# Cosine layer of a fused attention kernel: a step's seven products in one run and its twelve rows in the next, VectorE's chain work moved to the rows

## The chip, the cores and the metric

The kernel runs on one core of a Trainium2 chip. The metric is the device time of one execution in microseconds (us); before the change the median of three runs is 984.97 us (984.43 to 987.22). TensorE multiplies (PE in the profile, its weight loads PEld), VectorE (DVE) and ScalarE (ACT) work elementwise, GpSimd (POOL) too but only on SBUF, and SyncE (SP) issues the transfers.

## What is computed

```python
def reference(q, k, v, w_gate, w_val, w_out, w_in2, w_out2):
    x = sliding_window_attention(q, k, v)        # 4 x 8 heads, 576 tokens, window 128
    x = x.reshape(2304, 512)
    x = (silu(x @ w_gate) * (x @ w_val)) @ w_out # 512 -> 1536 -> 512
    h = x @ w_in2                                # 512 -> 2048: the cosine layer
    return ((h * cos(h)) @ w_out2).astype(float32)
```

All of it is float32. The kernel splits every operand of a product into a high and a low part and sums three matmuls (high x high, high x low, low x high).

## The kernel before

The kernel has three stages: attention (to about 230 us of the profile), the gated layer (to about 600 us) and the cosine layer (the last 380 us). The change touches the cosine layer alone.

**Steps.** The 2304 tokens are cut into NS = 3 stretches s of 768 columns, each stretch into two halves of 384. The 2048 columns of `w_in` are taken in 8 pairs p (NPAIR) of two blocks of 128. A step k = 8 s + p computes four blocks of h, (fi, half), from seven **products** m = 0 to 6 in place of eight (a scheme of the Strassen kind: the sums of inputs are made beforehand by `make_xt`, those of outputs by `take`). A product (`prod`, L1030 to L1032) is six matmuls of 384 columns, so a step has 42 of them. There are 24 steps, k = 0 to 23.

**Banks.** From the twelfth product on, a product writes one of the two banks of PSUM that the pool `pm` has (L196, `new_bank` L1114); product 6 goes on adding in the bank of product 4. So product m needs what product m - 2 left there to have been read.

**Emptying** (`take`, L1175, and `add`, L1171). Product 0 is copied by ScalarE (L1181), every other one is added to an earlier sum by VectorE (L1171). Four of the seven results, those of m = 1, 4, 5 and 6, are a finished block of h and start a **chain**.

**Chains** (`cosine`, L1142, a generator). One chain turns one block of 128 x 384 into h cos(h), high and low, in six parts: two operations of ScalarE that round (L1145, L1146); two of VectorE that give the remainder r (L1149, L1150); absolute value and sine on ScalarE (L1152, L1153); a multiplication on GpSimd (L1155); the high part on ScalarE (L1159); the low part on VectorE (L1161). `slot_chains` takes every living chain one part further after each product.

**Rows** (`out_rows`, L1206). The blocks of step k are multiplied by `w_out` in step k + 2: 12 rows (fi, j), each three matmuls of 512 columns (L84 to L86), 36 a step, which add into six banks over all eight steps of a stretch. The list `PER` says how many rows follow each product:

```python
    PER = [2, 2, 2, 2, 2, 1, 1]
```

**Inputs of the next stretch.** `make_xt` (L979) makes the seven inputs, high and low, of stretch s + 1 from the tile `raw`: operations 768 wide on ScalarE (L994), VectorE and GpSimd (both L991). In the kernel before they stand in a list `bg`, of which one is issued after each product from p = 3, m = 3 on. This happens twice, in steps 3 to 6 and 11 to 14.

**Queues.** Every engine runs its instructions in the order in which the program issues them; there is no planner here, so the order of the Python calls is the order of the engines. SyncE's queue carries the 256 KB of weights of each product (`load_ws`, seven buffers, seven products ahead), the two tiles of 512 KB for the rows (`load_wo`) and the outputs.

Of the kernel before, what the change touches and what calls it, by code (L numbers as in the profile page):

```python
# [13 lines left out]
ALU = mybir.AluOpType  # L14
# [14 lines left out]
def kernel(  # L29
# [50 lines left out]
    def f32(ap):  # L80
        return ap.bitcast(F32)
# [100 lines left out]
    post = deque()  # L182
# [25 lines left out]
    def flush():  # L208
        for _ in range(len(post)):
            post.popleft()()  # L210
# [768 lines left out]
    def make_xt(s, pool, raw):  # L979

        hi = [pool.tile([128, 2, BW], F32R, tag=f"xh{m}", name=f"xh{m}") for m in range(7)]
        lo = [pool.tile([128, 2, BW], F32R, tag=f"xl{m}", name=f"xl{m}") for m in range(7)]
        XT[s] = hi, lo
        b11, b12 = raw[:, 0:2, 0:BW], raw[:, 0:2, BW:SB]
        b21, b22 = raw[:, 2:4, 0:BW], raw[:, 2:4, BW:SB]

        src = [b11, b21, b11, b22, b12, b22, b21]
        v, g = nc.vector, nc.gpsimd

        def two(eng, out, a, b, op=ALU.subtract):  # L990
            return lambda: eng.tensor_tensor(out=out, in0=a, in1=b, op=op)  # L991

        def high(m):
            return lambda: nc.scalar.copy(out=hi[m], in_=src[m])  # L994

        def low(eng, m):
            return two(eng, lo[m], src[m], f32(hi[m]))
        return [
            high(0), high(1), two(g, b12, b22, b12), low(v, 0), low(v, 1), high(5), two(v, b11, b12, b11, ALU.add),
            low(g, 5), two(v, b21, b21, b11), high(2), high(4), two(g, b22, b22, b11), low(v, 2), high(6), low(v, 4),  # L1000
            high(3), low(v, 6), low(g, 3)]
# [140 lines left out]
    def cosine(k, fi, half, h):  # L1142

        a = ap_.tile([128, BW], F32, tag="a", name="a")
        nc.scalar.activation(out=a, in_=h, func=AF.Copy, scale=INV2PI, bias=MAGIC)  # L1145
        nc.scalar.activation(out=a, in_=a, func=AF.Copy, bias=-MAGIC)  # L1146
        yield
        r = rp.tile([128, BW], F32, tag="r", name="r")
        nc.vector.scalar_tensor_tensor(out=r, in0=a, scalar=-C1, in1=h, op0=ALU.mult, op1=ALU.add)  # L1149
        nc.vector.scalar_tensor_tensor(out=r, in0=a, scalar=-C2, in1=r, op0=ALU.mult, op1=ALU.add)  # L1150
        yield
        nc.scalar.activation(out=r, in_=r, func=AF.Abs)  # L1152
        nc.scalar.activation(out=r, in_=r, func=AF.Sin, bias=halfpi, scale=-1.0)  # L1153
        yield
        nc.gpsimd.tensor_tensor(out=r, in0=r, in1=h, op=ALU.mult)  # L1155
        yield
        hi = hp.tile([128, BW], F32R, tag="hh", name="hh")
        lo = hp.tile([128, BW], F32R, tag="hl", name="hl")
        nc.scalar.copy(out=hi, in_=r)  # L1159
        yield  # L1160
        (nc.vector if k else nc.gpsimd).tensor_tensor(out=lo, in0=r, in1=f32(hi), op=ALU.subtract)  # L1161
        HS[k, fi, half] = hi, lo

    def slot_chains(most):

        for c in list(live)[:most]:
            if next(c, "end") == "end":
                live.remove(c)

    def add(out, a, ps):  # L1170
        nc.vector.tensor_tensor(out=out, in0=ps[:, :BW], in1=a, op=ALU.add)  # L1171
# [3 lines left out]
    def take(k, m, ps):  # L1175

        def new(pool, tag):
            return pool.tile([128, BW], F32, tag=tag, name=tag)
        if m == 0:
            cur[k, "q"] = new(tp, "q")  # L1180
            nc.scalar.copy(out=cur[k, "q"], in_=ps[:, :BW])  # L1181
        elif m == 1:
            c = new(cp, "c")
            add(c, cur[k, "q"], ps)
            live.append(cosine(k, 0, 0, c))
        elif m == 2:
            add(cur[k, "q"], cur[k, "q"], ps)
        elif m == 3:
            cur[k, "r"] = new(tp, "r5")
            add(cur[k, "r"], cur[k, "q"], ps)  # L1190
        else:
            c = new(cp, "c")
            fi, half, base = {4: (1, 1, "r"), 5: (0, 1, "r"), 6: (1, 0, "q")}[m]
            add(c, cur[k, base], ps)
            live.append(cosine(k, fi, half, c))

    def load_wo(k):
        if k < K2:
# [3 lines left out]
                WO[k, fi] = t  # L1202

    sums = {}

    def out_rows(k, fi, j):  # L1206

        s, p = divmod(k, NPAIR)
        first, final = p == 0 and fi == 0, p == NPAIR - 1 and fi == 1
        if first:  # L1210
            sums[j] = (pl2.tile([128, 512], F32, tag="l2", name="l2") if j < 5 else
                       pl1a.tile([128, 512], F32, tag="l1", name="l1"))
        hi, lo = HS[k, fi, j // 3]
        w = WO[k, fi]
        c = slice(j % 3 * 128, (j % 3 + 1) * 128)
        mm3(sums[j], hi[:, c], lo[:, c], w[:, 0], w[:, 1], first, final)
        if final:
            def ev(ps=sums[j], row=s * 6 + j):
                o = op_.tile([128, 512], F32, tag="o", name="o")
                if j % 2 and s == NS - 1:  # L1220
                    nc.vector.tensor_copy(out=o, in_=ps)
                else:
                    nc.scalar.copy(out=o, in_=ps)
                nc.sync.dma_start(out=out[row * 128:(row + 1) * 128, :], in_=o)
            post.append(ev)

    raws = {}

    def load_raw(s):
        raws[s] = raw_p.tile([128, KD, SB], F32, tag="raw", name="raw")  # L1230
        nc.sync.dma_start(out=raws[s], in_=y2d[s])

    PER = [2, 2, 2, 2, 2, 1, 1]
    rows = deque()
    bg = deque()
    p7 = {}
    for at, (k, m) in enumerate(order):
        if k >= 2 and m == 0:
            pairs = [(fi, j) for fi in range(2) for j in range(6)]
            rows += [(k - 2, fi, j) for fi, j in (sorted(pairs, key=lambda x: x[1]) if k == K2 + 1 else pairs)]  # L1240
        if k < K2:
            if k == 0 and m < 2:
                ps = bank0[m]
            elif m == 6:
                ps = p7.pop(k)
                prod(k, m, ps, start=False)
            else:
                ps = new_bank(6 * k + m)
                prod(k, m, ps)
            if m == 4:  # L1250
                p7[k] = ps
        slot_chains(2 if k < 2 else 99)
        flush()
        if bg:
            bg.popleft()()
        if k < K2:
            take(k, m, ps)
        for _ in range(PER[m]):
            if rows:
                out_rows(*rows.popleft())  # L1260
        if k < K2:
            load_ws(at + 8)
        if m == 1:
            load_wo(k - 1 if k else K2)
        s, p = divmod(k, NPAIR)
        if k == 1 and m == 3:
            load_raw(1)
        if m == 3 and s + 1 < NS and p == 3:
            bg += make_xt(s + 1, xta if s % 2 else xtb, raws[s + 1])
        if m == 3 and s + 2 < NS and p == 6:  # L1270
            load_raw(s + 2)
    flush()
    sc.close()
    pre.close()
# [31 lines left out]
```

## Time and profile before

| | us |
|---|---|
| median of three runs | 984.97 (984.43 to 987.22) |
| the profiled execution, its own time | 982.86 |
| span of its profile | 981.1 |
| PE busy in the span | 958.9 (98%) |
| DVE, ACT, POOL busy | 735.7, 591.7, 483.8 |
| the chain that ended last: PE's share | 90% |

The span begins at the first instruction and ends with the last; the execution's own time has 1.8 us more around it. The busy time of PE is that of overlapping matmuls: one starts before the one ahead has ended. How fast TensorE goes is therefore read from the distance between starts, not from the durations. In the timeline each row has its start, how long it took, the engine, the source line, the operation and its tiles, out<-in; in brackets stands idle time just ahead of it and what ended that.

### The profile page before, as it was taken

The page shows a single profiled execution, that of the slowest core. Times are in us where ns is not written, and L with a number is a line of the kernel's source. Part 1 is how long each engine was busy: PE and PEld are TensorE (multiplying, and loading weights), DVE is VectorE, ACT ScalarE, POOL GpSimd, SP SyncE. Part 2 cuts the span into 40 slices and gives each one's busy share as a digit, 9 for nine tenths or more (in the row PEclk, how much of TensorE's full clock was granted, in tenths as well). Part 3 has the DMA queues.
Part 4 walks back from the last instruction along what each step waited for, and adds up shares of the span by engine and source line. Part 5 has one row for each costly group of instructions (what it writes and reads, how often), then busy time and mean ns, then how long its engine had stood idle before and what let it go on. Part 6 is the DMA issues. An engine that isn't in the chain of part 4 may idle for free.

```text
span 981.1 us, 16562 instructions
## 1 busy us (share of the span) xinstructions
PE 958.9 (98%) x5404; PEld 869.0 (89%) x5404; DVE 735.7 (75%) x1533; ACT 591.7 (60%) x1350; POOL 483.8 (49%) x555
## 2 busy tenths in 40 slices
PE   6889999999999999999999999999999999999998
PEld 4568877779999999999999999888889898898986
DVE  6877777766298989989889665898666896666664
ACT  6886665644254555555455324978667676776663
POOL 5666656462155668669678622545222442323221
PEclk9899999999999999999999999999999999999999
DMA  7641432321473647457467615866667656676552
GB/s 182 158 106 42 112 93 71 95 67 55 160 264 108 197 132 258 155 167 256 135 198 236 209 67 189 284 193 196 233 202 228 198 166 196 191 240 202 167 177 86
DMA packets 144005, 163.61 MB, mean 167 GB/s; under 512 B 64560, under 2 KB 103472, under 8 KB 143664
## 3 DMA queue, kind: packets, MB, share of 16 engines
q1 hardware_dynamic: 142720, 162.27, 52.9%
q8 instruction: 43, 0.70, 0.3%
q10 hardware_dynamic: 1200, 0.30, 0.1%
q14 instruction: 42, 0.34, 0.1%
HBM read 126.88 MB, written 35.65 MB: 166 GB/s over the span
## 4 chain that ended last, share of the span: by engine, by line
PE 90%; ACT 4%; DVE 3%; DMA 1%; issue 1%; SPq 1%; POOL 0%; DVEq 0%; POOLq 0%; ACTq 0%
PE l L86 13%; PE l L85 13%; PE l L84 13%; PE pm L84 8%; PE pm L86 8%; PE pm L85 8%; PE pm L1031 6%; PE pm L1032 6%; PE pm L1030 5%; PE s L515 3%; PE pv L634 2%; PE t L566 1%; PE pq L452 1%; ACT e L532 1%; DMA st<-in_moe_w_val_dram 1%
## 5 line engine op out<-in xcount | busy, mean ns | idle before, releaser
L1155 POOL TENSOR_TENSOR r<-r,c 128x384 f32<-128x384 f32 x96 | 104.9, 1094 | 249.4 <-ACT r L1153 165.3
L84 PE MATMUL pm<-xh,wh 128*128 128x384 f32 (+3 forms) x412 | 144.8, 352 | 1.6 <-ACT fu L263 1.6
L86 PE MATMUL pm<-xh,wl 128*128 128x384 f32 (+3 forms) x412 | 138.3, 336 | 0.0
L85 PE MATMUL pm<-xl,wh 128*128 128x384 f32 (+3 forms) x412 | 138.2, 335 | 0.0
L86 PE MATMUL l<-wo,hl 128*128 128x512 f32 x288 | 114.2, 396 | 0.0
L85 PE MATMUL l<-wo,hh 128*128 128x512 f32 x288 | 113.7, 395 | 0.0
L84 PE MATMUL l<-wo,hh 128*128 128x512 f32 x288 | 112.0, 389 | 1.6 <-DVE c L1171 1.6
L846 POOL TENSOR_TENSOR cs<-cs,st 128x512 uint32<-128x512 uint32 x56 | 80.3, 1434 | 57.2 <-DVE cs L844 49.6
L1031 PE MATMUL pm<-xl,ws 128*128 128x384 f32 x318 | 107.4, 338 | 0.0
L1032 PE MATMUL pm<-xh,ws 128*128 128x384 f32 x318 | 106.7, 336 | 0.0
L1030 PE MATMUL pm<-xh,ws 128*128 128x384 f32 x318 | 106.2, 334 | 0.0
L557 POOL TENSOR_SCALAR e<-e,st 128x128 f32<-128x128 f32 (+1 forms) x144 | 63.0, 440 | 57.6 <-DVE st L544 29.9
L84 PEld LDWEIGHTS pm<-xh,wh 128*128 128x128 f32 x412 | 77.6, 188 | 5.8 <-issue 2.8
L1145 ACT ACTIVATE a<-c 128x384 f32<-128x384 f32 x96 | 49.7, 518 | 53.2 <-DVE c L1171 53.2
L532 ACT ACTIVATE e<-e,st 128x256 f32<-128x256 f32 (+1 forms) x144 | 68.0, 474 | 19.9 <-DVE st L523 14.5
L86 PEld LDWEIGHTS pm<-xh,wl 128*128 128x128 f32 x412 | 77.3, 188 | 2.1
L1150 DVE SCALAR_TENSOR_TENSOR r<-a,r 128x384 f32<-128x384 f32 x96 | 76.7, 799 | 3.3
L85 PEld LDWEIGHTS pm<-xl,wh 128*128 128x128 f32 x412 | 77.6, 188 | 0.4
L1152 ACT ACTIVATE r<-r 128x384 f32<-128x384 f32 x96 | 50.4, 525 | 42.0 <-DVE r L1150 42.0
L84 PE MATMUL l<-uh,wh 128*128 128x384 f32 x216 | 72.5, 336 | 0.6 <-DVE acc L971 0.5
L86 PE MATMUL l<-uh,wl 128*128 128x384 f32 x216 | 72.2, 334 | 0.0
L85 PE MATMUL l<-ul,wh 128*128 128x384 f32 x216 | 72.2, 334 | 0.0
(177 smaller groups left out, 2569.3 us busy)
## 6 DMA issues: line engine op xcount, KB each, us to landing
ws<-wid SPq DMA_DIRECT2D x168, 256.0 KB, 2.9
wo<-wod SPq DMA_DIRECT2D x48, 512.0 KB, 5.3
st<-in_moe_w_out_dram SPq DMA_DIRECT2D x28, 512.0 KB, 4.0
st<-in_moe_w_in_dram SPq DMA_DIRECT2D x16, 512.0 KB, 3.7
st<-in_moe_w_gate_dram SPq DMA_DIRECT2D x12, 512.0 KB, 4.4
st<-in_moe_w_val_dram SPq DMA_DIRECT2D x12, 512.0 KB, 3.9
wid<-sh SPq DMA_DIRECT2D x24, 256.0 KB, 4.2
wid<-sl SPq DMA_DIRECT2D x24, 256.0 KB, 3.5
```

Of the source, the lines that this page charges most:

```text
L84: nc.tensor.matmul(out=ps, lhsT=ah, rhs=bh, start=start, stop=False)
L85: nc.tensor.matmul(out=ps, lhsT=ah, rhs=bl, start=False, stop=False)
L86: nc.tensor.matmul(out=ps, lhsT=al, rhs=bh, start=False, stop=stop)
L532: nc.scalar.activation(out=e[:, :w], in_=e[:, :w], func=AF.Exp, bias=st[:, m:m + 1], scale=-1.0, accum_out=st[:, 2 + 2 * m:3 + 2 * m])
L557: nc.gpsimd.tensor_scalar(e[:, :w], e[:, :w], st[:, 8 + m:9 + m], 1.0, ALU.mult, ALU.mult)
L846: nc.gpsimd.tensor_tensor(out=ti, in0=ti, in1=st[:, :, 0], op=ALU.add)
L1030: nc.tensor.matmul(out=o, lhsT=wh, rhs=xh_, start=start and kk == 0, stop=False, skip_group_check=True)
L1031: nc.tensor.matmul(out=o, lhsT=wh, rhs=xl_, start=False, stop=False, skip_group_check=True)
L1032: nc.tensor.matmul(out=o, lhsT=wl, rhs=xh_, start=False, stop=kk == 1, skip_group_check=True)
L1150: nc.vector.scalar_tensor_tensor(out=r, in0=a, scalar=-C2, in1=r, op0=ALU.mult, op1=ALU.add)
L1152: nc.scalar.activation(out=r, in_=r, func=AF.Abs)
L1155: nc.gpsimd.tensor_tensor(out=r, in0=r, in1=h, op=ALU.mult)
```

## The change

Steps 0 to 2 keep their order. From step 3 (`LONG`) to step 23 a step issues its seven products one after the other and then its twelve rows. The chains are no longer taken one part further per product; two new functions say which parts are due at each product (`beside_products`) and at each row (`beside_rows`):

```diff
+    class Chain:
+        def __init__(self, k, place, *args):
+            self.k, self.place, self.done, self.ops = k, place, 0, cosine(k, *args)
+        def step(self):
+            self.done += 1
+            next(self.ops, None)
+            if self.done == 6:
+                live.remove(self)
...
+    def beside_products(k, m):
+        late = 3 if k == LONG else 0
+        for c in list(live):
+            x = c.place
+            if c.k < k - 1:
+                due = 6
+            elif c.k == k - 1:
+                due = sum((m >= x or x == 3, m >= x or x == 3, m >= (late if x == 3 else x),
+                           m >= (late + 1 if x == 3 else x), m >= x + 1 + late // 2))
+                due = 0 if m < x and late else due
+            else:
+                due = 0
+            while c.done < due:
+                c.step()
+
+    def beside_rows(k, i):
+        for c in list(live):
+            x = c.place
+            if c.k < k - 1:
+                due = 6
+            elif c.k == k - 1:
+                due = 6 if i >= x // 2 else 5
+            else:
+                due = sum((i >= x, i >= x + 2, i >= x + 4 and x < 3, i >= x + 5 and x < 3))
+            while c.done < due:
+                c.step()
...
+        if m == 0 and LONG <= k < K2 and p == 3 and s + 1 < NS:
+            parts = make_xt(s + 1, xta if s % 2 else xtb, raws[s + 1])
+        if LONG <= k < K2:
             take(k, m, ps)
-        for _ in range(PER[m]):
-            if rows:
+            beside_products(k, m)
+            if rows_out and m:
+                rows_out.popleft()()
+            if m == 5 and parts:
+                for op in parts[0][0]:
+                    op()
+            for i in range(12 if m == 6 else 0):
+                beside_rows(k, i)
                 out_rows(*rows.popleft())
+            if m == 6 and parts:
+                for op in parts.popleft()[1]:
+                    op()
```

So in a settled step VectorE does, beside the products, the six adds; beside the rows the four low parts of the step before and the four pairs of r operations of the step itself. Of GpSimd's four multiplications three are issued beside the rows and one (place 3, the chain of product 6) beside the next step's products. `make_xt` comes in five parts, one a step in steps 3 to 7 and 11 to 15: ScalarE's operations at product 5, those of VectorE and GpSimd behind the twelfth row. Six of the outputs' copies at a stretch's end are issued one per product, and `raw` of the last stretch is loaded in step 8. In steps 24 and 25, where only rows are left, the order is as before. Every instruction keeps its size, and none is added or left out. In the changed kernel L1149, L1150, L1155, L1161 and L1171 stand at L1156, L1157, L1162, L1168 and L1217.

TensorE, step 3, from the second half of product 5 on, before (`ws` are a product's weights, `wo` those of a row, `pm` the products' banks, `l2` those of the rows):

```order
L1030 MATMUL pm_7766<-xh5_6830,ws_7603 128x384
L1031 MATMUL pm_7766<-xl5_6837,ws_7603 128x384
L1032 MATMUL pm_7766<-xh5_6830,ws_7603 128x384
L84 MATMUL l2_7489<-wo_7497,hh_7563 128x512
L85 MATMUL l2_7489<-wo_7497,hh_7563 128x512
L86 MATMUL l2_7489<-wo_7497,hl_7564 128x512
L1030 MATMUL pm_7742<-xh6_6831,ws_7623 128x384
L1031 MATMUL pm_7742<-xl6_6838,ws_7623 128x384
L1032 MATMUL pm_7742<-xh6_6831,ws_7623 128x384
```

and now:

```order
L1037 MATMUL pm_7721<-xh5_6830,ws_7603 128x384
L1038 MATMUL pm_7721<-xl5_6837,ws_7603 128x384
L1039 MATMUL pm_7721<-xh5_6830,ws_7603 128x384
L1037 MATMUL pm_7706<-xh6_6831,ws_7623 128x384
L1038 MATMUL pm_7706<-xl6_6838,ws_7623 128x384
L1039 MATMUL pm_7706<-xh6_6831,ws_7623 128x384
```

The row that stood between product 5 and product 6 is gone from there; now the products of a step follow each other, and its twelve rows follow product 6.

VectorE in step 3, from the add of its product 1 on, before:

```order
L1171 TENSOR_TENSOR c_7664<-pm_7651,q_7641 128x384
L1171 TENSOR_TENSOR q_7641<-pm_7678,q_7641 128x384
L1161 TENSOR_TENSOR hl_7686<-r_7615,hh_7685 128x384
L1149 SCALAR_TENSOR_TENSOR r_7715<-a_7691,c_7664 128x384
L1150 SCALAR_TENSOR_TENSOR r_7715<-a_7691,r_7715 128x384
L1171 TENSOR_TENSOR r5_7718<-pm_7703,q_7641 128x384
L1161 TENSOR_TENSOR hl_7712<-r_7635,hh_7711 128x384
L1171 TENSOR_TENSOR c_7756<-pm_7742,r5_7718 128x384
L1161 TENSOR_TENSOR hl_7751<-r_7661,hh_7750 128x384
L1171 TENSOR_TENSOR c_7779<-pm_7766,r5_7718 128x384
L1149 SCALAR_TENSOR_TENSOR r_7795<-a_7775,c_7756 128x384
```

and now, from the add of step 2's last product (`c_7621`) to that of step 3's last (`c_7743`):

```order
L1217 TENSOR_TENSOR c_7621<-pm_7555,q_7432 128x384
L1217 TENSOR_TENSOR c_7657<-pm_7650,q_7646 128x384
L1217 TENSOR_TENSOR q_7646<-pm_7668,q_7646 128x384
L1156 SCALAR_TENSOR_TENSOR r_7676<-a_7618,c_7598 128x384
L1157 SCALAR_TENSOR_TENSOR r_7676<-a_7618,r_7676 128x384
L1217 TENSOR_TENSOR r5_7691<-pm_7684,q_7646 128x384
L1156 SCALAR_TENSOR_TENSOR r_7699<-a_7696,c_7621 128x384
L1157 SCALAR_TENSOR_TENSOR r_7699<-a_7696,r_7699 128x384
L1217 TENSOR_TENSOR c_7713<-pm_7706,r5_7691 128x384
L1217 TENSOR_TENSOR c_7728<-pm_7721,r5_7691 128x384
L1217 TENSOR_TENSOR c_7743<-pm_7706,q_7646 128x384
```

`c`, `q` and `r5` on the left of L1171 and L1217 are adds that empty a bank; `r` is the remainder of a chain, `hl` a low part. In step 3, the first with the new order, the pairs of two chains of step 2 (`r_7676`, `r_7699`) stand among the adds of products that now follow each other; from step 4 on the adds stand by themselves.

VectorE at the end of step 4 and the start of step 5, now:

```order
L1156 SCALAR_TENSOR_TENSOR r_7951<-a_7934,c_7902 128x384
L1157 SCALAR_TENSOR_TENSOR r_7951<-a_7934,r_7951 128x384
L1156 SCALAR_TENSOR_TENSOR r_7960<-a_7943,c_7913 128x384
L1157 SCALAR_TENSOR_TENSOR r_7960<-a_7943,r_7960 128x384
L991 TENSOR_TENSOR raw_7379<-raw_7379 128x2x384
L1217 TENSOR_TENSOR c_8013<-pm_8006,q_8000 128x384
L1217 TENSOR_TENSOR q_8000<-pm_8025,q_8000 128x384
L1217 TENSOR_TENSOR r5_8045<-pm_8038,q_8000 128x384
L1217 TENSOR_TENSOR c_8059<-pm_8052,r5_8045 128x384
```

and GpSimd at the same place, now:

```order
L1162 TENSOR_TENSOR r_7931<-r_7931,c_7842 128x384
L1162 TENSOR_TENSOR r_7940<-r_7940,c_7888 128x384
L1162 TENSOR_TENSOR r_7951<-r_7951,c_7902 128x384
L991 TENSOR_TENSOR xl1_7640<-raw_7379,xh1_7633 128x768
L991 TENSOR_TENSOR xl5_7644<-raw_7379,xh5_7637 128x768
L1162 TENSOR_TENSOR r_7960<-r_7960,c_7913 128x384
```

`raw_7379` on VectorE, `xl1_7640` and `xl5_7644` on GpSimd are operations of `make_xt`, 768 wide; the four `r` of GpSimd are the multiplications of step 4's chains. VectorE's 768-wide operation now stands between the last pair of the rows and the first add of the next products, where GpSimd issues its own.

## Rows read from the trace of the kernel before

**Rows 1.** windows: busy us of PE, PEld, DVE, ACT, POOL, then clock, DMA.
```profile
630.00:960.00 330.00, 330.00 (x1644) 296.69 (x1643) 238.64 (x397) 236.30 (x471) 106.97 (x92) 1.00 0.62 196
```

**Rows 2.** timeline, PEld, 16 steps or 1248 starts apart.
```profile
708.01 0.19 PEld L1030 LDWEIGHTS pm<-xh,ws 128*128 128x128 f32 x1
...
959.00 0.19 PEld L1030 LDWEIGHTS pm<-xh,ws 128*128 128x128 f32 x1
```

**Rows 3.** timeline, PEld, products alone, 71 starts apart.
```profile
600.76 0.19 PEld L1030 LDWEIGHTS l<-xh,ws 128*128 128x128 f32 x1
...
613.06 0.19 PEld L1032 LDWEIGHTS pm<-xh,ws 128*128 128x128 f32 x1
```

**Rows 4.** timeline, PEld, rows alone, 59 starts apart.
```profile
962.93 0.19 PEld L84 LDWEIGHTS l<-wo,hh 128*128 128x128 f32 x1
...
976.30 0.19 PEld L86 LDWEIGHTS l<-wo,hl 128*128 128x128 f32 x1
```

**Rows 5.** timeline, a product's last matmul, its add, and the next load behind an add.
```profile
720.04 0.33 PE L1032 MATMUL pm<-xh,ws 128*128 128x384 f32 x1
...
720.41 0.56 DVE L1171 TENSOR_TENSOR c<-pm,r 128x384 f32<-128x384 f32 x1 [1.41 <-PE pm L1032]
...
805.22 0.55 DVE L1171 TENSOR_TENSOR c<-pm,q 128x384 f32<-128x384 f32 x1
...
805.82 0.19 PEld L1030 LDWEIGHTS pm<-xh,ws 128*128 128x128 f32 x1
```

**Rows 6.** tile r, 630 to 960 us: duration ns min/median/max, first and last start us, forms.
```profile
L1161 DVE TENSOR_TENSOR hl<-r,hh x85: 543/548/2085, 630.3 to 956.2; 128x384 fp32r<-128x384 f32 x85
L1149 DVE SCALAR_TENSOR_TENSOR r<-a,c x85: 542/550/1368, 630.7 to 958.6; 128x384 f32<-128x384 f32 x85
L1150 DVE SCALAR_TENSOR_TENSOR r<-a,r x85: 557/558/2253, 631.3 to 959.2; 128x384 f32<-128x384 f32 x85
L1152 ACT ACTIVATE r<-r x85: 517/526/537, 631.9 to 959.8; 128x384 f32<-128x384 f32 x85
L1153 ACT ACTIVATE r<-r,halfpi x84: 615/617/621, 632.5 to 953.5; 128x384 f32<-128x384 f32 x84
L1171 DVE TENSOR_TENSOR c<-pm,r x43: 544/557/558, 629.8 to 958.2; 128x384 f32<-128x384 f32 x43
```

**Rows 7.** tiles hh, a and raw, the same columns.
```profile
L1159 ACT CAST hh<-r x85: 494/498/526, 629.5 to 957.3; 128x384 fp32r<-128x384 f32 x85
...
L1146 ACT ACTIVATE a<-a x85: 524/526/528, 630.9 to 959.3; 128x384 f32<-128x384 f32 x85
...
L991 DVE TENSOR_TENSOR raw<-raw x4: 944/947/948, 657.2 to 785.8; 128x768 f32<-128x768 f32 x4
```

**Rows 8.** timeline, VectorE and GpSimd on the same tiles' memory at one time.
```profile
654.96 1.86 POOL L991 TENSOR_TENSOR xl<-raw,xh 128x768 fp32r<-128x768 f32 x1 [0.90 <-DVE r L1149]
...
654.98 2.25 DVE L1150 SCALAR_TENSOR_TENSOR r<-a,r 128x384 f32<-128x384 f32 x1
...
805.68 0.54 DVE L1161 TENSOR_TENSOR hl<-r,hh 128x384 fp32r<-128x384 f32 x1
...
805.71 1.39 POOL L1155 TENSOR_TENSOR r<-r,c 128x384 f32<-128x384 f32 x1 [1.70 <-ACT r L1153]
...
741.82 0.56 DVE L1150 SCALAR_TENSOR_TENSOR r<-a,r 128x384 f32<-128x384 f32 x1
742.77 0.90 DVE L1149 SCALAR_TENSOR_TENSOR r<-a,c 128x384 f32<-128x384 f32 x1 [0.39 <-ACT a L1146]
```

**Rows 9.** timeline, ScalarE's sine and GpSimd's multiplication that waits for it.
```profile
729.46 0.62 ACT L1153 ACTIVATE r<-r,halfpi 128x384 f32<-128x384 f32 x1
...
730.21 1.01 POOL L1155 TENSOR_TENSOR r<-r,c 128x384 f32<-128x384 f32 x1 [0.46 <-ACT r L1153]
...
668.87 0.62 ACT L1153 ACTIVATE r<-r,halfpi 128x384 f32<-128x384 f32 x1
...
669.57 1.29 POOL L1155 TENSOR_TENSOR r<-r,c 128x384 f32<-128x384 f32 x1 [0.41 <-ACT r L1153]
```

More of the change, by code (lines that the diff above doesn't have):

```diff
@@ L997, in low @@
             return two(eng, lo[m], src[m], f32(hi[m]))
+        if s:
+            return deque([
+                ([high(0), high(1)], [two(g, b12, b22, b12), low(v, 0)]),
+                ([high(5)], [low(g, 1), two(v, b11, b12, b11, ALU.add), low(g, 5)]),
+                ([high(2), high(4)], [two(v, b21, b21, b11), two(g, b22, b22, b11)]),
+                ([high(6), high(3)], [low(v, 2), low(g, 4)]),
+                ([], [low(v, 6), low(g, 3)])])
         return [
@@ L1162, in cosine @@
         HS[k, fi, half] = hi, lo
+    class Chain:
[6 more added lines that the diff above has]
+                live.remove(self)
     def slot_chains(most):
         for c in list(live)[:most]:
-            if next(c, "end") == "end":
-                live.remove(c)
+            c.step()
[23 more added lines that the diff above has]
+            while c.done < due:
+                c.step()
     def add(out, a, ps):
@@ L1184, in take @@
             add(c, cur[k, "q"], ps)
-            live.append(cosine(k, 0, 0, c))
+            live.append(Chain(k, 0, 0, 0, c))
         elif m == 2:
@@ L1194, in take @@
             add(c, cur[k, base], ps)
-            live.append(cosine(k, fi, half, c))
+            live.append(Chain(k, m - 3, fi, half, c))
     def load_wo(k):
@@ L1204 @@
     sums = {}
+    LONG = 3
     def out_rows(k, fi, j):
@@ L1224, in ev @@
                 nc.sync.dma_start(out=out[row * 128:(row + 1) * 128, :], in_=o)
-            post.append(ev)
+            (rows_out if s < NS - 1 else post).append(ev)
     raws = {}
+    rows_out = deque()
     def load_raw(s):
@@ L1233 @@
     PER = [2, 2, 2, 2, 2, 1, 1]
+    parts = deque()
     rows = deque()
-    bg = deque()
     p7 = {}
@@ L1251 @@
                 p7[k] = ps
[L1252 to L1256, printed above, removed]
-            take(k, m, ps)
-        for _ in range(PER[m]):
-            if rows:
-                out_rows(*rows.popleft())
+        s, p = divmod(k, NPAIR)
+        if m == 0 and LONG <= k < K2 and p == 3 and s + 1 < NS:
+            parts = make_xt(s + 1, xta if s % 2 else xtb, raws[s + 1])
+        if LONG <= k < K2:
+            take(k, m, ps)
+            beside_products(k, m)
[6 more added lines that the diff above has]
+                beside_rows(k, i)
+                out_rows(*rows.popleft())
+            if m == 6 and parts:
+                for op in parts.popleft()[1]:
+                    op()
+        else:
+            while rows_out:
+                rows_out.popleft()()
+            slot_chains(2 if k < 2 else 99)
+            flush()
+            if k < K2:
+                take(k, m, ps)
+            for _ in range(PER[m]):
+                if rows:
+                    out_rows(*rows.popleft())
         if k < K2:
@@ L1264 @@
             load_wo(k - 1 if k else K2)
-        s, p = divmod(k, NPAIR)
         if k == 1 and m == 3:
             load_raw(1)
[L1268 to L1271, printed above, removed]
+        if m == 3 and 0 < s < NS - 1 and p == 0:
+            load_raw(s + 1)
     flush()
```

## Prediction

> **What bounds the kernel now.** I read the table of busy time first, then the cosine layer in the windows view, then its timeline, then the tiles of the chains. In the windows view TensorE is busy for all of 330 us, at the clock's upper level (1.00, 2.4 GHz), while VectorE works 239 of 330 us and GpSimd 107 [rows 1]. So the time of this stage is the distance between TensorE's starts; other engines count only where they make a start late. Sixteen steps take 959.00 - 708.01 = 250.99 us [rows 2], 15.69 us a step. The profile also has stretches of one kind: products alone start every 12.30 / 71 = 0.1733 us [rows 3], rows alone every 13.37 / 59 = 0.2266 us [rows 4]. A step made of these would take 42 x 0.1733 + 36 x 0.2266 = 15.44 us. The reader is to see the 0.25 us between: it goes to the seven places a step where products and rows alternate, 0.036 us each.
>
> The second thing to see is how tight a bank is. A product's add starts 0.37 us after the start of its last matmul (720.04 to 720.41) [rows 5] and takes 0.56; the load that needs the bank starts 0.05 after it ends (805.77 to 805.82) [rows 5]. From a product's first load to its last matmul's start are 6 x 0.173 = 1.04 us, so a bank is free again 1.04 + 0.37 + 0.56 + 0.05 = 2.02 us after its product began. With rows between the products nobody waits for that; in a run of products the bank is wanted after 12 x 0.1733 = 2.08. **An add may be 0.06 us late; whatever is beyond that, TensorE waits.**
>
> The third is what holds VectorE up. Its operations with both inputs in SBUF (L1149, L1150, L1161) take 0.55 in the median and up to 2.25; the adds, with one input in PSUM, never more than 0.56 [rows 6]. The long ones are those that met GpSimd: L1150 began 0.02 behind a 768-wide operation of GpSimd (654.96, 1.86 us) and ended 0.41 after it [rows 8], so it began its own 0.56 us when GpSimd was all but done. The other way round GpSimd takes 1.39 in place of 1.01 [rows 8, 9].
>
> **The change, part by part.** No operation is added or removed, so only order costs or gives.
>
> *Regrouping.* 21 steps (3 to 23) go from seven alternations to one. The one that stays costs at least the 0.036 of today; at most I take twice that, since the runs around it are longer. With 0.055, a step takes 15.50, and 21 x (0.25 - 0.055) = **-4.0 us** (bounds -3.7 and -4.5). Here a rule speaks against the change. The Trainium skill, page "TensorE: Matmul & The Clock Gate", section "Back-to-back issue gap", gives the gap between matmuls as a function of their own columns alone (N / 2.4 + 2.5 ns at the upper clock); by it the order of products and rows gives nothing, this term would be 0 and the sum 4.0 higher. The rows differ: 0.1733 where it has 0.1625, and a mixed step longer than its parts.
>
> *The first step of the new order, k = 3.* In the old order chains are behind: when step 3's products come, two pairs of chains of step 2 stand among the adds. (a) The add of step 2's product 6 is behind a pair (0.55 + 0.03 + 0.56): it starts about 0.5 late, and product 1 waits **0.45** (bounds 0 and 0.7, since it hangs on how far VectorE is then). (b) The pair `r_7676` is between the adds of products 2 and 3; these then start 0.47 + 1.14 - 0.08 = 1.53 apart (an operation that needs nothing from the one ahead starts 0.08 before its end), not 1.04, so the second is 0.49 late, and product 5 waits **0.43**. (c) The pair `r_7699` is ahead of the add of product 4, whose bank product 6 needs, and it waits for ScalarE. ScalarE, in its order, must first do absolute value and sine of `r_7676`, a high part, and the two roundings. From the end E of the first pair: 0.03 + 0.53 + 0.03 + 0.62 + 0.40 (0.50, of which 0.10 overlaps) + 0.43 + 0.03 + 0.53 = 2.60 [rows 6, 7], then the pair 0.03 + 0.55 + 0.03 + 0.56, and the add, begun 0.08 before the pair's end, 0.56: E + 4.24, the load at E + 4.29. Product 5 began at E + 0.53, so product 6 was due at E + 1.57: it waits **2.7**. Together +3.6 us (bounds 0.5, if ScalarE were far ahead, and 4).
>
> *Steps with `make_xt`.* The adds of a settled step stand alone among the products, 1.04 apart, and keep the 0.06. But VectorE's load in the rows is its chain work: product 6's add, four low parts, four pairs: 0.84 + 4 x 0.47 + 4 x 1.06 = 6.96 of the 8.2 us of twelve rows. Three multiplications of GpSimd are there too, and each time VectorE meets one it loses 0.7 to 0.8: with three meetings the last pair ends 1.1 to 1.2 us into the next products. That alone harms nothing: product 1's add is due at 2.45. In nine steps (4 to 7, 11 to 15) 768-wide operations of both engines come next. If GpSimd's is first, it holds VectorE's for 1.57 (1.86 without the 0.14 at either end in which VectorE isn't held), VectorE's own takes 0.95 [rows 7], and the add of product 1 ends 1.2 + 1.57 + 0.95 - 0.08 + 0.56 = 4.2 us into the products. Product 3, due at 3.15, waits **1.1 us**. If VectorE's is first, the add is in time.
>
> Who is first? Let T be the end of VectorE's third pair. GpSimd's second multiplication gets the memory at T, VectorE's next operation waits behind it until T + 1.29 (742.38 to 743.67) [rows 8], and its last one starts at T + 1.32. GpSimd's third multiplication waits for ScalarE, T + 0.03 + 0.53 + 0.03 + 0.62, and then starts 0.13 later or 0.08 later; the trace has both (730.08 to 730.21, 669.49 to 669.57) [rows 9]. Which it is goes with where the program puts the wait: 0.08 where the multiplication itself carries it, 0.13 where a waiting instruction ahead of it does. In the changed program that is 0.08 in steps 6 and 14 and 0.13 in the other seven. So in two steps GpSimd starts 0.04 ahead and wins, **+2.2 us**; in seven VectorE starts 0.01 to 0.02 ahead. In the rows a lead of 0.02 to 0.03 decides, on either side (654.96 and 654.98; 805.68 and 805.71) [rows 8]; a lead of 0.01 is not shown. I take VectorE as the winner there, cost 0, with the other end at 7 x 1.1 = 7.7 us. The Trainium skill, page "SBUF — State Buffer", section "Who interferes with whom", says that whoever issues first gets the port pair for the whole instruction; by that rule even 0.01 would do, and the seven cost nothing.
>
> *At no cost.* Weights of a product are loaded seven products ahead, which is still a whole step, and SyncE's queue waits for nothing new for long. ScalarE, 236 of 330 us [rows 1], has its operations in the same number. The copies of finished rows, one per product, precede by 2 us or more the rows that need the bank. The small waits of today (0.05 in a few steps) go: -0.2. If these covers failed, each is worth a few tenths in two or three steps.
>
> **Sum**, against the profiled execution's own 982.86: -4.0 + 3.6 + 2.2 - 0.2 = +1.6; I round the regrouping down for waits of some hundredths that the tight banks leave in single steps and take +2.1, 985.0. The median of the runs stands 2.1 above the profiled execution, so 984.97 + 2.1 = **987.1 us**.
>
> **Rivals.**
> 1. *GpSimd wins the seven close races too* (slower). It decides at the end of the rows of steps 4, 5, 7, 11 to 13 and 15; from a lead of about 0 on. All of them: 987.1 + 7.7 = 994.8, and 995.3 with what the later steps lose in turn; some of them: 989 to 993. For it: the lead is smaller than any the trace shows, and one hundredth more of waiting turns it. Against: every VectorE operation that began first in the trace got through.
> 2. *The new waits stay away* (faster). If ScalarE is further ahead in step 3 than its order of work says, (c) shrinks to nothing, and if VectorE is some tenths earlier at the rows' end, the two certain collisions go too: 984.97 - 4.0 = 981.0. One of the two alone gives 983.4 to 984.9, no change. Against: (c) is a chain of fixed durations in a fixed order.
> 3. *The 0.25 us a step are not the alternation's* but belong to what the other engines do beside it, and stay, as the first rule has it. Then +3.6 + 2.2 alone: 990.8. For it: the rows alone [rows 4] are from the end, where the others do little. Against: the products alone [rows 3] are from a place where they work, and are as far below the mixed step.
> 4. That the change doesn't do what it says: the order shows that it does, so no chance.
>
> **How the numbers follow.** A measurement of this kernel can tell about 0.3%, 3 us, from no change. The forecast (986 to 988.5) has 0.49; rival 1 in full 0.19, in part 0.11; rival 2 in full 0.08, by half 0.08; rival 3 0.05. Faster by over 0.3% (below 982.0) is rival 2 in full: 0.08. Slower (above 987.9) are rivals 1 and 3, and the forecast's upper edge: 0.19 + 0.11 + 0.05 + 0.02 = 0.37. The rest, 0.55, is within. The range takes in the forecast, rival 1 whole, rival 3 and most of rival 2's half: 983.8 to 996; the forecast's own is 986 to 988.5.
>
> **What would show it.** In the new profile: loads of products 0.173 apart within a step, of rows 0.227, and a step of 15.50 us from first load to first load in steps 17 to 23, where neither `make_xt` nor step 3 is. One wait of TensorE of 2.7 us ahead of product 6 of step 3, behind an add, and two of 0.4 before it. Waits of 1.1 us ahead of product 3 in steps 7 and 15, with VectorE's L991 at 2.6 us; in the other seven steps with `make_xt`, L991 at 1.4 or less and no wait. It is wrong if L991 is long in all nine, if step 3 has no long wait, or if settled steps take over 15.6 us.

## The result, and the profile after

The changed kernel takes 997.09 us in the median of five runs (996.41 to 998.70), the kernel before 984.43 beside it (983.02 to 987.22): a ratio of 1.0132 with an interval of 1.0113 to 1.0152, slower by 1.3%. The forecast was 987.1, within 983.8 to 996.0. The profiled execution of after is that of 996.41 us, its span 994.7.

| profiled execution, us | before | after |
|---|---|---|
| own time | 982.86 | 996.41 |
| span | 981.1 | 994.7 |
| PE busy in the span | 958.9 | 962.3 |
| cosine layer, first to last weight load | 379.71 | 393.37 |
| PE's share of the chain that ended last | 90% | 87% |

The windows view of the cosine layer, to be read beside [rows 1] (columns as there):

```profile
630.00:960.00 330.00, 320.71 (x1585) 287.16 (x1584) 237.07 (x381) 229.44 (x457) 123.08 (x95) 0.99 0.56 194
```

TensorE, busy for all of 330 us before, now stands still for over 9 of them, and the granted clock is no longer 1.00. VectorE and ScalarE are no busier than before (237 and 229 us against 239 and 236), so it is a question of who waits for whom. GpSimd is busy for 16 us more, and the views of L991, before and then after, show a part of the change that is not order:

```profile
L991 DVE TENSOR_TENSOR xl<-raw,xh x10: 945/947/1306, 648.9 to 804.3; 128x768 fp32r<-128x768 f32 x10
L991 POOL TENSOR_TENSOR xl<-raw,xh x4: 1855/1880/1921, 655.0 to 802.1; 128x768 fp32r<-128x768 f32 x4
```

```profile
L991 POOL TENSOR_TENSOR xl<-raw,xh x8: 1842/2356/2573, 668.2 to 846.2; 128x768 fp32r<-128x768 f32 x8
L991 DVE TENSOR_TENSOR xl<-raw,xh x6: 1768/1776/2599, 651.3 to 845.3; 128x768 fp32r<-128x768 f32 x6
```

Four operations of `make_xt` (`xl1` and `xl4`, in both stretches) went from VectorE to GpSimd. The new order itself did what was forecast. A settled step, from first row to first row, or first product to first product (timeline of after, PEld):

```profile
896.30 0.19 PEld L1037 LDWEIGHTS pm<-xh,ws 128*128 128x128 f32 x1
903.66 0.19 PEld L84 LDWEIGHTS l<-wo,hh 128*128 128x128 f32 x1
911.81 0.19 PEld L1037 LDWEIGHTS pm<-xh,ws 128*128 128x128 f32 x1
919.17 0.19 PEld L84 LDWEIGHTS l<-wo,hh 128*128 128x128 f32 x1
```

It takes 15.51 us both ways, against 15.69 before [rows 2].

All the loss is waits of TensorE, and what follows some of them. Its loads after idle time, the same view (in brackets the idle time and what ended it), from step 3 to step 10:

```profile
633.89 0.19 PEld L1037 LDWEIGHTS pm<-xh,ws 128*128 128x128 f32 x1 [0.27 <-DVE c L1217]
638.42 0.19 PEld L1037 LDWEIGHTS pm<-xh,ws 128*128 128x128 f32 x1 [0.41 <-DVE r L1217]
642.19 0.19 PEld L1037 LDWEIGHTS pm<-xh,ws 128*128 128x128 f32 x1 [2.77 <-DVE c L1217]
702.23 0.19 PEld L1037 LDWEIGHTS pm<-xh,ws 128*128 128x128 f32 x1 [1.08 <-DVE c L1217]
718.36 0.19 PEld L1038 LDWEIGHTS pm<-xl,ws 128*128 128x128 f32 x1 [0.46 <-POOL xl L991]
758.72 0.19 PEld L84 LDWEIGHTS l<-wo,hh 128*128 128x128 f32 x1 [2.67 <-ACT o L1270]
760.01 0.20 PEld L84 LDWEIGHTS l<-wo,hh 128*128 128x128 f32 x1 [0.76 <-ACT o L1270]
```

The first three are step 3, the fourth is product 3 of step 7; both were forecast. The fifth is product 3 of step 8, which waits for `xl3`, the last operation of `make_xt`; the last two are rows of step 10. Those two kinds were not forecast. The fourth, the fifth and the rows' waits come again eight steps on, at 832.69, 848.85 and 888.90.

**What the rows of step 10 wait for** is seen from three queues. ScalarE, the copies of finished rows (L1270):

```profile
752.05 0.59 ACT L1270 COPY o<-l 128x512 f32<-128x512 f32 x1
758.09 0.58 ACT L1270 COPY o<-l 128x512 f32<-128x512 f32 x1 [5.45 <-DMA out_dram<-o]
759.37 0.58 ACT L1270 COPY o<-l 128x512 f32<-128x512 f32 x1 [0.70 <-DMA out_dram<-o]
```

The first four of the six run one after the other; the fifth waits 5.45 us for a transfer of an output to land. Its pool has three buffers. SyncE's queue at that place:

```profile
749.95 0.34 SPq L1271 DMA_DIRECT2D out_dram<-o  x1
750.38 0.38 SPq L1027 DMA_DIRECT2D ws<-wid  x1
750.81 0.92 SPq L1247 DMA_DIRECT2D wo<-wod  x2
751.83 0.38 SPq L1271 DMA_DIRECT2D out_dram<-o  x1
```

The 1 MB of `wo` is issued between the first and the second output. And the tile view of `o`, its last line, before and then after:

```profile
DMA to landing us min/median/max: 2.0/2.1/2.8
```

```profile
DMA to landing us min/median/max: 2.0/3.1/6.2
```

The second output, issued at 751.83, lands 6.2 us later, at 758.0, and at 758.09 the fifth copy begins.

**What follows the wait** is the clock. Loads behind the second wait (timeline), and the granted clock there (windows view, the last but two of its columns):

```profile
760.94 0.33 PEld L84 LDWEIGHTS l<-wo,hh 128*128 128x128 f32 x1
761.37 0.33 PEld L85 LDWEIGHTS l<-wo,hh 128*128 128x128 f32 x1
761.79 0.33 PEld L86 LDWEIGHTS l<-wo,hl 128*128 128x128 f32 x1
```

```profile
760.30:763.50 3.20, 3.20 (x9) 2.43 (x9) 2.46 (x5) 3.07 (x8) 0.00 (x0) 0.50 0.81 295
```

A clock of 0.50 is the lower level, 1.2 GHz; rows start 0.427 us apart in place of 0.227 [rows 4]. The same happens behind the wait of step 18 and behind that of step 2's first row, which was there before (1.94 us) and is 2.21 now. The windows behind those two waits, and then the one behind step 2's wait in the kernel before, where the clock stayed up:

```profile
891.00:893.50 2.50, 2.50 (x7) 1.95 (x7) 2.29 (x5) 2.40 (x7) 0.00 (x0) 0.55 0.95 334
616.50:620.20 3.70, 3.70 (x13) 3.29 (x11) 2.15 (x4) 3.60 (x9) 1.03 (x2) 0.54 0.98 400
```

```profile
615.30:620.30 5.00, 5.00 (x25) 4.47 (x26) 3.37 (x7) 4.87 (x11) 1.90 (x3) 1.00 1.03 417
```

The account, from the distances between loads (what a distance has beyond 0.173 for a product, 0.227 for a row): regrouping 21 x (15.69 - 15.51) = -3.7; step 3, 0.29 + 0.42 + 2.79 = +3.5; product 3 of steps 7 and 15, +2.2; `xl3` in steps 8 and 16, +1.0; rows of steps 10 and 18, (2.63 + 0.72) + (2.39 + 0.71) = +6.5; the lower clock at three places, 1.54 + 1.57 + 1.37 = +4.5; step 2's wait, +0.3. Together +14.3, against 393.37 - 379.71 = +13.7. The difference is mostly this: behind a wait the next load comes 0.06 us (product) or 0.12 us (row) sooner than in an undisturbed run, some 0.8 us over all waits, which the sum doesn't count.

### The profile page after: what moved, and what is told of

It reads as the page before. It is cut to its first block, busy times and chain, and to the rows that moved or that the text cites. A ratio compares the mean times of both kernels' runs of the same rounds, so it can differ in the third digit from the quotient of the medians.

```text
span 994.7 us, 16539 instructions
## 1 busy us (share of the span) xinstructions
PE 962.3 (97%) x5404; PEld 872.0 (88%) x5404; DVE 738.9 (74%) x1529; ACT 591.3 (59%) x1350; POOL 502.0 (50%) x559
## 4 chain that ended last, share of the span: by engine, by line
PE 87%; DVE 5%; DMA 3%; ACT 2%; issue 1%; SPq 1%; POOL 1%; POOLq 0%; DVEq 0%; ACTq 0%
PE l L84 13%; PE l L86 12%; PE l L85 12%; PE pm L84 8%; PE pm L86 8%; PE pm L85 8%; PE pm L1037 5%; PE pm L1038 5%; PE pm L1039 5%; PE s L515 3%; PE pv L634 3%; DMA out_dram<-o 1%; PE pq L452 1%; PE t L576 1%; PE t L566 1%
## 5 line engine op out<-in xcount | busy, mean ns | idle before, releaser
L1162 POOL TENSOR_TENSOR r<-r,c 128x384 f32<-128x384 f32 x96 | 112.6, 1176 | 248.2 <-ACT r L1160 206.1
L84 PE MATMUL l<-wo,hh 128*128 128x512 f32 x288 | 114.2, 396 | 6.8 <-ACT o L1270 4.9
L85 PE MATMUL l<-wo,hh 128*128 128x512 f32 x288 | 113.9, 396 | 0.0
L1156 DVE SCALAR_TENSOR_TENSOR r<-a,c 128x384 f32<-128x384 f32 x96 | 67.6, 704 | 16.9 <-ACT a L1153 16.9
L1157 DVE SCALAR_TENSOR_TENSOR r<-a,r 128x384 f32<-128x384 f32 x96 | 69.5, 724 | 3.3
```

The lines of the kernel that those rows point to most:

```text
L84: nc.tensor.matmul(out=ps, lhsT=ah, rhs=bh, start=start, stop=False)
L85: nc.tensor.matmul(out=ps, lhsT=ah, rhs=bl, start=False, stop=False)
```

## Experiments

Every ratio is to the kernel before, run on the same chip. The changed kernel's is 1.0132.

### More buffers for the copies, and fewer for r

```diff
-    rp = ... name="rp", bufs=8
-    op_ = ... name="op", bufs=3
+    rp = ... name="rp", bufs=6
+    op_ = ... name="op", bufs=6
```

> Six buffers instead of three for the copies of finished rows (o); r gets six instead of eight to make room. Theory A: the fifth and sixth copy of steps 10 and 18 wait for a buffer of o, whose transfer lands 6.2 us after its issue; the rows wait for the copies (3.35 us in step 10, 3.10 in step 18), and TensorE's half clock behind them (1.4 and 1.25 us) follows from the wait. Then both go: 997.1 - 9.1 = 988.0 us, no load of L84 waits for L1270, clock 1.00 in both stretches. Theory B: the copies come late because of their place in ScalarE's queue; buffers change nothing: 996 to 998. Theory C: the clock falls there for a reason of its own; only the waits go: 990.6.

Measured: 994.79 us, ratio 1.0117 (1.0092 to 1.0143). The time alone would speak for theory B; the trace doesn't. In the tile view of `o`, the line on waiting for a transfer and those on engines that waited for `o` are gone:

```profile
its engine sat idle before it (us, times) until:
  PE l L86: 20.8, 6
who waited for it (us, times):
busy tenths in 40 slices 0000000000000000000000000000001000010001
DMA to landing us min/median/max: 2.0/5.1/6.7
```

The transfers still take up to 6.7 us, but nobody waits for them, and behind steps 10 and 18 the clock stays at its upper level. What is new are waits ahead of product 3 in nine steps (5 to 8 and 12 to 16) in place of two, 1.08 to 1.10 us each: 9.8 us where waits on `make_xt` had been 3.2. Theory A is right on the copies, and the second size in the edit turned the races of `make_xt`; the next kernels take the two sizes apart.

### The weights of the rows behind the outputs

```diff
-        if m == 1:
+        if m == (6 if LONG <= k < K2 and p == 2 else 1):
             load_wo(k - 1 if k else K2)
```

> Three buffers as they were; in steps 10 and 18 the two tiles of wo (1 MB) are issued behind product 6 instead of behind product 1, so behind the outputs. If the transfers of o land late because the 1 MB is ahead of them, they land some 3 us after their issue now, the copies come in time and the time is 988 to 989. If three buffers are too few however the queue stands, the waits stay: 995 to 998.

Measured: 989.43 us, ratio 1.0068 (1.0043 to 1.0092), some 6 us less than the changed kernel. In step 10 one wait of 0.79 us is left of 3.35, in step 18 none, and the clock stays up behind both. The fifth copy begins 2.1 us after the fourth in place of 6.0; the sixth still waits 2.15 us for a buffer (timeline, ACT):

```profile
753.05 0.59 ACT L1270 COPY o<-l 128x512 f32<-128x512 f32 x1
755.17 0.59 ACT L1270 COPY o<-l 128x512 f32<-128x512 f32 x1 [1.54 <-DMA out_dram<-o]
757.91 0.58 ACT L1270 COPY o<-l 128x512 f32<-128x512 f32 x1 [2.15 <-DMA out_dram<-o]
```

Product 2 of steps 11 and 19 now waits 0.62 and 0.54 for ScalarE's copy; that the late sixth copy is what delays ScalarE there is likely and was not tried. Even so placed, an output takes up to 5.3 us to land, so the 1 MB ahead of the outputs is most of the cause, and three buffers leave no room for the rest.

### make_xt without VectorE

```diff
-                ([high(0), high(1)], [two(g, b12, b22, b12), low(v, 0)]),
+                ([high(0), high(1)], [two(g, b12, b22, b12), low(g, 0)]),
...
-                ([], [low(v, 6), low(g, 3)])])
+                ([], [low(g, 3), low(g, 6)])])
```

> VectorE's ten 768-wide operations of make_xt go to GpSimd, in the same steps; in the last part xl3 is made ahead of xl6. If the waits of 1.1 us ahead of product 3 of steps 7 and 15 are VectorE held by GpSimd's 768-wide operation, and those of 0.5 in steps 8 and 16 wait for xl3, both go: 997.1 - 2.2 - 1.0 = 993.9 us. Rival: GpSimd then has 1.85 us more in each of ten steps, holds the pairs of r in the next rows or delivers xl3 and xl6 late: 995 to 999, with waits behind L991 on GpSimd.

Measured: 993.75 us, ratio 1.0111 (1.0089 to 1.0132). The four waits are gone, and no wait on GpSimd's L991 takes their place. By the ratio the gain is 2 us and not 3.2. In the profiled execution the rows' waits for the copies are longer than in the changed kernel's (2.90 + 0.72 and 2.98 + 0.71), and product 2 of step 11 waits 0.62 behind them; why the outputs land later there was not tried.

### The two chains of step 3

```diff
+                if late and x == 2:
+                    due = sum((m >= 0, m >= 0, m >= 2, m >= 2, m >= 4))
+                if late and x == 3:
+                    due = sum((m >= 1, m >= 5, m >= 6, m >= 6))
...
+                if k == LONG and x == 3:
+                    due = sum((i >= 5, i >= 6), 4)
```

> In step 3 alone: the pair of r of step 2's chain of place 2 goes ahead of the add of product 1, where VectorE idles; the chain of place 3 has its roundings at product 1, its pair behind the add of product 5, its sine at product 6 and the rest in the rows. If the waits ahead of products 5 and 6 (0.42 and 2.79 us) are the pairs among the adds, they go and 0.3 ahead of product 1 stays: 997.1 - 3.2 = 993.9. Rival: ScalarE, which has the sine and two wide copies more to do at product 6, brings the copy of step 4's product 0 late: a new wait of 1 us or more in step 4, 995 to 996.

Measured: 993.39 us, ratio 1.0111 (1.0084 to 1.0139). The waits ahead of products 5 and 6 are gone, and step 4 has no new one. VectorE's adds now stand by themselves (timeline):

```profile
635.07 0.56 DVE L1223 TENSOR_TENSOR r<-pm,q 128x384 f32<-128x384 f32 x1 [0.48 <-PE pm L1039]
636.10 0.56 DVE L1223 TENSOR_TENSOR c<-pm,r 128x384 f32<-128x384 f32 x1 [0.48 <-PE pm L1039]
637.14 0.56 DVE L1223 TENSOR_TENSOR c<-pm,r 128x384 f32<-128x384 f32 x1 [0.48 <-PE pm L1039]
637.62 0.55 DVE L1156 SCALAR_TENSOR_TENSOR r<-a,c 128x384 f32<-128x384 f32 x1
```

In this execution the wait ahead of step 2's first row was shorter (0.83 us in place of 2.21), and products 0 and 1 of step 3 waited 0.70 and 1.00 for VectorE: the sum is 2.53 here and 2.50 in the changed kernel.

### More buffers for the copies, with r as it was

```diff
-    ap_ = ... name="ap", bufs=4
-    op_ = ... name="op", bufs=3
+    ap_ = ... name="ap", bufs=3
+    op_ = ... name="op", bufs=5
```

> Five buffers for o, the room taken from the tile a (three in place of four), which leaves every wait of GpSimd as it is in the changed kernel. Theory A, told apart from the races: the waits of steps 10 and 18 (3.35 and 3.10 us) and the half clock behind them (1.57 and 1.37) go, the waits ahead of product 3 stay two of 1.1 us (steps 7 and 15): 9.4 less than the changed kernel, a ratio to before of 1.0037 (988 where before has 984.4). Rival: the nine races were lost in the first run because the earlier copies shift VectorE, not because of r's buffers; then nine waits of 1.1 us again and a ratio of 1.012.

Measured: 987.36 us, ratio 1.0046 (1.0030 to 1.0062), within 0.1% of what theory A gave. No row waits for a copy, and the clock stays up behind steps 10 and 18. The rest is not as expected. No race is lost, and the two waits of steps 7 and 15, which were to stay, are gone as well: VectorE begins its L991 some 0.5 us ahead of the step's products in most steps, where in the changed kernel's close races it began 0.35 to 0.44 behind their start. `xl3` is late by 0.65 us in step 8 and again in step 16. So the fit of the time to 0.1% is in part luck, and as this edit too has two sizes in it, it shows the cause of the copies' waits and not that of VectorE's earlier start.

### Fewer buffers for r alone

```diff
-    rp = ... name="rp", bufs=8
+    rp = ... name="rp", bufs=6
```

> Of the first run's two sizes only the second: six buffers for r in place of eight, three for o as they were. Theory: it alone decides the races, since GpSimd's third multiplication of a step then carries its wait itself and begins 0.03 ahead of VectorE in place of 0.02 behind it. Then nine waits of 1.1 us ahead of product 3 in place of two, the two of 0.5 behind product 3 go, the waits of steps 10 and 18 stay: 7 x 1.1 - 1.0 = 6.7 us more than the changed kernel, ratio to before 1.020. Rival: in the first run the races were lost because the copies came earlier; then ratio 1.013 and two such waits.

Measured: 1002.57 us, ratio 1.0191 (1.0168 to 1.0215); nine waits of 1.10 us, the copies' waits where they were and up to 0.4 us longer. It is rival 1 of the prediction, in full. The same place, the start of step 5, in the changed kernel:

```profile
666.85 0.56 DVE L1157 SCALAR_TENSOR_TENSOR r<-a,r 128x384 f32<-128x384 f32 x1
667.32 1.77 DVE L991 TENSOR_TENSOR raw<-raw 128x768 f32<-128x768 f32 x1
669.48 0.56 DVE L1217 TENSOR_TENSOR c<-pm,q 128x384 f32<-128x384 f32 x1 [0.39 <-PE pm L1039]
...
666.86 1.42 POOL L1162 TENSOR_TENSOR r<-r,c 128x384 f32<-128x384 f32 x1 [0.46 <-POOL r L1162]
668.24 2.57 POOL L991 TENSOR_TENSOR xl<-raw,xh 128x768 fp32r<-128x768 f32 x1
```

and with six buffers for r, where GpSimd's 768-wide operations (two in one row) begin ahead of VectorE's:

```profile
666.88 1.38 DVE L1157 SCALAR_TENSOR_TENSOR r<-a,r 128x384 f32<-128x384 f32 x1
668.19 2.60 DVE L991 TENSOR_TENSOR raw<-raw 128x768 f32<-128x768 f32 x1
670.71 0.54 DVE L1217 TENSOR_TENSOR c<-pm,q 128x384 f32<-128x384 f32 x1
...
666.84 1.01 POOL L1162 TENSOR_TENSOR r<-r,c 128x384 f32<-128x384 f32 x1 [0.41 <-DVE r L1156]
667.81 4.68 POOL L991 TENSOR_TENSOR xl<-raw,xh 128x768 fp32r<-128x768 f32 x2
```

In the changed kernel VectorE's L1157 begins 0.01 us ahead of GpSimd's multiplication and gets through in 0.56, while GpSimd takes 1.42. With six buffers the multiplication begins 0.08 us after ScalarE's sine has ended, in place of 0.13, and so 0.04 ahead; VectorE's then takes 1.38 and everything behind it is late. That the 0.05 are those of a wait that the multiplication now carries itself is the prediction's reading of its [rows 9]; the run shows that the buffer count alone sets it.

### Three edits in one

Six buffers for `o` and for `r`, `make_xt` on GpSimd, step 3's chains as above.

> Three edits in one: six buffers for o and six for r, make_xt's ten operations on GpSimd, the new places of step 3's two chains. If the parts add up, the waits of steps 10, 18, 7, 15, 8, 16 and of products 5 and 6 of step 3 are all gone: 9.4 + 3.2 + 3.2 less a wait of 1 us or so at the start of step 3: 14.8 less than the changed kernel, ratio 0.998. If the races come back in another form (GpSimd's 768-wide operation holding the pairs of r in the rows until the adds are late), ratio 1.003 to 1.008 with waits ahead of product 3.

Measured: 980.80 us, ratio 0.9976 (0.9965 to 0.9986). This version is faster than both kernels. From step 3 on a single wait is left in the cosine layer, 0.52 us ahead of product 1 of step 3, and the windows view reads

```profile
630.00:960.00 330.00, 329.82 (x1656) 298.74 (x1655) 239.41 (x391) 239.09 (x480) 134.20 (x108) 1.00 0.57 197
```

The parts add up: 14.8 us less than the changed kernel was expected, and the ratios differ by 0.0156, which is 15.3 us. Everything that the changed kernel lost from step 3 on has a cause that can be taken away, and what stays is the regrouping.

### The wait ahead of step 2's first row

Four kernels try to take that wait away; it is in the kernel before, too.

```diff
-        if m == 1:
-            load_wo(k - 1 if k else K2)
-        if k == 1 and m == 3:
+        if (k, m) == (0, 5) or k > 1 and m == 1:
+            load_wo(k - 1 if k else 0)
+        if k == 2 and m == 1:
             load_raw(1)
```

> The same and the first rows' weights issued at product 5 of step 0 in place of product 1 of step 1, raw behind the next step's. If the wait of 2.2 us ahead of step 2's first row is for that transfer and nothing else is late there, it goes, and what VectorE is behind (0.7 and 1.0 us at products 0 and 1 of step 3 where that wait was 0.8) grows by up to 0.8: 1 to 2 us less than without this edit, ratio 0.9965. If VectorE is the bound up to step 3, the wait only moves: no gain, ratio 0.998.

> The kernel before with the same earlier transfer alone. There chains lag but nothing waits for them product by product: the wait of 1.9 us ahead of step 2's first row goes, ratio 0.998. If VectorE is the bound, ratio 1.000.

Measured: ratios 0.9977 (0.9967 to 0.9988) and 1.0004 (0.9995 to 1.0013): no gain in either. The wait only moves from the rows' weights to those of step 1's product 6, here with the three edits (timeline, PE):

```profile
615.11 0.41 PE L1037 MATMUL pm<-xh,ws 128*128 128x384 f32 x1 [2.46 <-DMA ws<-wid]
```

In the kernel before with the same edit that product waits 0.93 us, for the same transfer, and product 0 of step 3 waits 0.62 for VectorE. The DMA engines are at a share of 1.01 from 602 to 615 us in the first and of 0.98 in the second: they have hardly any room left, so another order of the transfers makes another one late. The times are those of the second alternatives, but the wait that is left ahead of product 6 is one for a transfer and not for VectorE.

```diff
         prod(0, m, bank0[m])
+    load_ws(9)
     second(K - 1)
```

> The kernel with three edits, and the weights of the eighth and ninth product issued ahead of the last four outputs of the gated layer, which held SyncE's queue until 602 us. If the wait ahead of step 2's first row (2.0 us) is one for the transfers as a whole, started too late, it shrinks by 1 to 1.5 us and the one at step 3 grows by some tenths: ratio 0.9968. If those transfers have no room in the queues before 602 either, no change: 0.9976.

In the next kernel, beside that, `(nc.vector if k else nc.gpsimd)` at L1168 becomes `k > 1`.

> The same, and the four low parts of step 1's chains on GpSimd, which takes 4 x 0.47 from VectorE in step 2. If VectorE is what is behind at the start of step 3, the wait of 0.5 us ahead of product 1 goes as well: ratio 0.996. If GpSimd's operations hold VectorE's instead, no gain or 0.5 us lost: 0.9968 to 0.9975.

Measured: ratios 0.9975 (0.9962 to 0.9987) and 0.9977 (0.9966 to 0.9988), against 0.9976 without. In the first the wait ahead of the rows does fall to 0.63, but products 0 and 1 of step 3 now wait 0.91 and 1.00; in the second product 5 of step 2 and product 1 of step 3 wait 0.54 and 1.71. With the wait ahead of the rows (1.97, 0.63 and 0.69) and the one of 0.52 at step 3 that the version without has, the waits of steps 2 and 3 come to 2.5, 2.5 and 2.9 us: when the weights come earlier, VectorE is as much behind. The changed kernel and the six experiments ahead of the one with three edits show the same: the wait ahead of the rows runs from 0.83 to 2.21 us, and with those ahead of products 0 and 1 of step 3 it comes to 2.47 to 2.53 in every one. Moving four operations to GpSimd did not help it.

## Why the prediction was wrong

**Regrouping, -4.0: right,** -3.7. A settled step takes 15.51, forecast 15.50. Rival 3 falls, and the rule of the Trainium skill ("TensorE: Matmul & The Clock Gate", "Back-to-back issue gap"), a formula that the page gives for an isolated matmul and by which the order of products and rows gives nothing, does not describe this trace.

**Step 3, +3.6: right,** +3.5: 0.29, 0.42 and 2.79 for 0.45, 0.43 and 2.7. The experiment on that step's chains takes the last two away. The 0.29 is in part luck: it is what step 2's wait of 2.21 us leaves of some 2.5, and in the kernel with the later `wo`, where that wait is 1.13, products 0 and 1 of step 3 wait 1.39, beyond the forecast's bound of 0.7.

**make_xt, two certain collisions, +2.2: right** in place and price, 1.10 each at product 3 of steps 7 and 15. The operation of GpSimd that holds VectorE there is `xl4`, one of the four that the change moved from VectorE, so this term is not one of order alone, as the prediction has it. The seven close races went to VectorE, as taken: five with leads of 0.01 to 0.02, two (steps 5 and 13) by 0.9, its L991 against GpSimd's third multiplication (682.06 and 682.97 in step 5); that this was a near thing the kernel with six buffers for r shows, whose nine waits of 1.1 are rival 1. VectorE's L991 was forecast at 1.4 or less in the seven; it takes 1.77, held by GpSimd's multiplication, and its add still comes in time (669.48, where it waits for TensorE). The rule taken from the Trainium skill, page "SBUF — State Buffer", "Who interferes with whom", agrees with the five races: the one that began first, by 0.01 to 0.02, got through.

**"At no cost" is the step that failed.** It said that the copies of finished rows, one per product, precede by 2 us or more the rows that need the bank, and that SyncE's queue waits for nothing new for long. That set the copies' place in ScalarE's order against the rows, and left out what a copy itself needs: one of three buffers, free only when an earlier output has landed, and that output's place in SyncE's queue, behind 1 MB of `wo`. If this cover failed, the prediction priced it at a few tenths in two or three steps; it cost 3.35 and 3.10 us in two. Before, the copies began in the middle of the step ahead (734.43), were spread over 8 us (to 742.64), and their transfers took at most 2.8. The cost is +6.5 us; its cause is shown by five buffers (1.0046), with which no row waits for a copy, and by the later `wo` (1.0068).

**No term for the clock.** The profile before has 1.00 in all of this stage, and the sum took each wait at its own length. Behind the long ones TensorE then ran at 1.2 GHz for some 3 us: +4.5 us in all. The two drops behind the copies went when the copies' waits went, with five buffers, with six and with the later `wo`.

**No term for `xl3`, +1.0.** The prediction followed VectorE's part of `make_xt` and not GpSimd's last operation: it ends 3.8 us into the products of step 8, while the second matmul of product 3 wants it some 3.4 us in.

So the three terms of the sum came to +2.0 measured, where the prediction had +1.8 (+2.1 with its small waits and its rounding); what it left out came to +12. The step that was cheapest to write, a sentence for what costs nothing, hid half of that by itself, and three quarters with the clock behind it. Slower had a chance of 0.37 in the prediction, but by rivals 1 and 3 and the forecast's upper edge, and none of these is what made it slower.

What stays open: where the drop behind step 2's wait comes from was not tried by itself, since none of the kernels takes that wait away without moving it. In four of the experiments (six buffers for both, the later `wo`, five buffers, six for r alone) it is absent, and one behind step 3's long wait is there in its place.

## What to carry to other kernels

When an operation is moved, list everything that it needs to start: not only its operands and its place in its own queue, but the buffer that it writes, who frees that, and what stands ahead of the freeing transfer in its queue. A stage that is paced by one engine can lose time behind a wait as well as in it (here 1.1 to 1.6 us behind waits of 2.1 to 3.2), so a long wait has a second price. And an experiment with two sizes in it should be read from the trace: here one edit gave back 9 us and lost 7 elsewhere, and its time looked like no effect.

## What the runs showed of the hardware

- **The clock after a wait.** Over the profiles of this case, none of TensorE's waits of up to 2.02 us in the cosine layer was followed by the lower level; of 17 waits of 2.1 to 3.2 us 13 were. The same wait of 2.79 ahead of product 6 of step 3 was followed by it in the first kernel with more buffers and not in the changed kernel. A drop cost 1.1 to 1.6 us.
- **Hundredths decide, and repeat.** Where VectorE and GpSimd both want SBUF, a lead of 0.01 to 0.02 us of VectorE's held in five races of the changed kernel, and 0.04 the other way lost all nine with six buffers for r. What set it was a buffer count, by which the multiplication began 0.08 or 0.13 us after the sine that it waits for.
- **Transfers under load.** An output of 256 KB landed 2.0 us after its issue where the queues were free and up to 8.1 us after it beside 1 MB of weights (the kernel with five buffers), where nobody waited for it.
